# The last 64 rows of the contraction in the weight gradients gw2 and gw1 as paired 64-row matmuls

## The chip, the cores and the metric

The kernel runs on one core of one Trainium2 chip. The core has a matrix engine (PE, with weight loads shown apart as PEld), a vector engine (DVE), a scalar engine (ACT), GpSimd (POOL), a queue engine for transfers (SP), and 16 DMA engines. The metric is the device time of one execution in microseconds (us). Before the change it is 370.83 us, the median of three runs (369.65 to 373.05).

## The reference

One block of a spectral token mixer and a token MLP, forward and backward. `x` is 2048 tokens by 448 channels (d), all in bf16. Eight arrays come out: the forward result and seven gradients.

```
h  = x + irfft2(rfft2(layernorm(x)) * (w_r + i w_i))
v  = layernorm(layernorm(h))                  # the MLP norms its input again
u  = gelu(einsum("bsd,sf->bdf", v, w1) + b1)  # F = 1792
y  = einsum("bdf,fs->bds", u, w2) + b2
h2 = h + transpose(y)
outputs: h2 and the gradients of x, w_r, w_i, w1, b1, w2, b2
```

The two gradients that matter here are sums over the 448 channels:

- gw2 (`out_6`, 1792 x 2048): gelu output (f by d) times the incoming gradient (d by s).
- gw1 (`out_4`, 2048 x 1792): normed input (s by d) times the gradient ahead of the gelu (d by f).

## The kernel before

[...] 448 is three times 128 plus 64. Both gradients take the channels in four chunks of 128 rows. `ld_t4` (L187) loads a transposed operand in two DMAs: chunks 0 to 2 hold d 0 to 383, chunk 3 holds d 320 to 447, so that its first 64 rows repeat d 320 to 383. In one operand of each product those 64 rows are set to zero by a memset on POOL (`g_t` at L658, `du_t` at L712), so that they add nothing. An output tile of 128 x 512 is thus four matmuls of full height, the last of them half zeros.

The stages, with the times of the profiled execution: the forward spectral part, with the products of w2 and the incoming gradient (`dg`, L442) between its matmuls (to about 108 us); w1 with the gelu (L523, to 139); w2 (L591, to 182); the product with w1 backwards and its layernorm, sixteen blocks (L647, `norm_back`, to 228); the backward spectral part (228 to 332), in which gw2 and the first six blocks of gw1 lie between its matmuls; the rest of gw1 (332 to 364).

`gw2(j, on)` computes 128 rows of gw2: four output tiles n = 0 to 3, four matmuls each (L666). The letters of `on` say who copies each tile from PSUM to the buffer `s6`: "a" is ACT, "v" is DVE. It is "aaaa" for j = 0 and "aaav" for j = 1 to 13. Then a DMA of POOL's queue stores the rows. gw1 is sixteen blocks of the same form (L730 to L742), with three tiles of 512 columns and one of 256, all copied by ACT; the last block is stored in four pieces by SP.

The backward spectral part is a chain: `fft_rows` (L315), `fft_cols` (L333 to L347, then DVE sums L353, then L325 to L327), the complex products `cmul` on DVE (L366 to L369), `ifft_cols` (L383, L384, ACT copies L400, DVE sums L402 and L404), and `ifft_rows` with `norm_back` for sixteen rows (L413 to L422, ACT L616, DVE L619 to L622). A product of the weight gradients for w_r and w_i (`grad_w`) runs on DVE behind gw1's fourth block.

PSUM buffers come from two rings: `ps_mm` with 3 (L163: `dg`, gw2, gw1, the w1 product backwards, half of the gelu blocks) and `ps_sp` with 5 (L166: all spectral tiles, the other half). The w2 stage takes four tiles at a time from both (L588).

The order of the instructions on each engine is fixed when the program is built. A planner goes through ready instructions by priority, which is program order unless the program raises it, and gives a tile its buffer when one is free by its own estimate of the times. The backward spectral part stands ahead of gw2's blocks 1 to 13 and of gw1 in the program, so that these fill what the chain leaves. `tc.issue_after(ins)` keeps what is written under it behind `ins` on that engine's queue. On the chip each engine then runs its queue in order and waits at semaphores.

Of the kernel before, what the change touches and what calls it, by code (L numbers as in the profile page):

```python
# [17 lines left out]
P = 128  # L18
S = 2048
D = 448  # L20
# [3 lines left out]
NT = 16  # L24
# [89 lines left out]
def kernel(  # L114
# [20 lines left out]
    nc = tc.nc  # L135
    ve, ac, po, pe = nc.vector, nc.scalar, nc.gpsimd, nc.tensor
# [16 lines left out]
    def k1(shape, name, dtype=BF16):  # L153
        return ring.tile(shape, dtype, tag="k1", bufs=10, name=name)
# [5 lines left out]
        return ring.tile([P, n], dtype, tag=name, bufs=4, name=name)  # L160

    def ps_mm(shape, dtype=F32):
        return psum.tile(shape, dtype, tag="mm", bufs=3, name="ps_mm")  # L163

    def ps_sp(shape, dtype=F32):
        return psum.tile(shape, dtype, tag="sp", bufs=5, name="ps_sp")  # L166

    def ld(out, in_, eng=None):
        return (eng or nc.sync).dma_start(out=out, in_=in_)

    def st(out, in_, eng=None):
        return (eng or po).dma_start(out=out, in_=in_)  # L172

    def ld_t(out, in_):
        return nc.sync.dma_start(out=out, in_=in_, transpose=True)
# [11 lines left out]
    def ld_t4(out, in_):  # L187

        ld_t(out[:, 0:3, :], in_[:, 0:384])
        ld_t(out[:, 3, :], in_[:, 320:448])  # L190

    def ev(out, in_, on):
        if on == "a":
            return ac.copy(out=out, in_=in_)  # L194
        return ve.tensor_copy(out=out, in_=in_)
# [4 lines left out]
    def rows(ap):  # L200
        return ap.rearrange("(q h) d -> q h d", h=NT)
# [157 lines left out]
    def cmul(out, a, b, conj, done=None):  # L359
        for r0, r1 in R_GROUPS:  # L360
            n = (r1 - r0) * DF
            sl = slice(r0 * DF, r1 * DF)
            t_r = e4([P, 2, n], "t_r")
            t_i = e4([P, 2, n], "t_i")
            o_r, o_i = out(r0, r1)
            ve.tensor_tensor(out=t_r[:], in0=a[:, :, sl], in1=b[:, 0:1, sl].broadcast_to([P, 2, n]), op=ALU.mult)  # L366
            ve.tensor_tensor(out=t_i[:], in0=a[:, :, sl], in1=b[:, 1:2, sl].broadcast_to([P, 2, n]), op=ALU.mult)  # L367
            ve.tensor_tensor(out=o_r, in0=t_r[:, 0, :], in1=t_i[:, 1, :], op=ALU.add if conj else ALU.subtract)
            last = ve.tensor_tensor(out=o_i, in0=t_r[:, 1, :], in1=t_i[:, 0, :],  # L369
                                    op=ALU.subtract if conj else ALU.add)  # L370
            if done is not None:
                done(r0, r1, last)
# [201 lines left out]
    for c, sl in enumerate((0, 2, 4, 6)):  # L574
# [4 lines left out]
        t = slot(sl, [P, NFB, 512], f"w2c{c}")  # L579
# [5 lines left out]
    for t0 in range(0, NT, 4):  # L585
        hr = e4([P, 4, D], "hr")
        ld(hr[:], hn_d.rearrange("(t p) d -> p t d", p=P)[:, t0:t0 + 4, :], po)
        p2 = [ps([P, D]) for ps in ((ps_sp, ps_sp, ps_sp, ps_mm), (ps_sp, ps_sp, ps_mm, ps_mm))[t0 // 4 % 2]]  # L588
        for j in range(NFB):
            for i in range(4):  # L590
                pe.matmul(p2[i][:], lhsT=w2c[t0 // 4][:, j, i * P:(i + 1) * P], rhs=gT[:, j, :],  # L591
                          start=(j == 0), stop=(j == NFB - 1))
        for i in range(4):
            t = t0 + i
            h2 = k1([P, D], "h2")
            ve.scalar_tensor_tensor(out=h2[:], in0=p2[i][:], scalar=b2col[:, t:t + 1], in1=hr[:, i, :],  # L596
                                    op0=ALU.add, op1=ALU.add)
            h2_last = st(out_0[0][t * P:(t + 1) * P, :], h2[:])
# [31 lines left out]
    for h in range(NT):  # L630
# [3 lines left out]
        if h == 4:  # L634
            goT = slot(4, [P, 4, S], "goT")
# [7 lines left out]
        with tc.issue_after(chain[-1].ins):  # L643
            w1T_last = ld_t(w1T[:], w1Tv[h])
# [9 lines left out]

    g_t = slot(0, [P, 4, F], "g_t")
    ld_t4(g_t[:], gT_d[:])
    with tc.issue_after(h2_last.ins):
        po.memset(g_t[0:64, 3, :], 0.0)  # L658
    first = []

    def gw2(j, on):
        s6 = w4([P, S], "s6")
        for n in range(4):
            pw = ps_mm([P, 512])
            for c in range(4):
                mm = pe.matmul(pw[:], lhsT=g_t[:, c, j * P:(j + 1) * P], rhs=goT[:, c, 512 * n:512 * n + 512],  # L666
                               start=(c == 0), stop=(c == 3))
            ev(s6[:, 512 * n:512 * n + 512], pw[:], on[n])
        first.append(mm)
        return st(out_6[j * P:(j + 1) * P, :], s6[:])  # L670

    gw2(0, "aaaa")
    fft_rows(dh, zt2, 3, "aava", first[0])
    ds = slot(3, [P, 2, XW], "ds")
# [24 lines left out]
    st(out_7.rearrange("(q h) -> q h", h=NT), gb2b[:])  # L699

    for j in range(1, NFB):
        s6_st = gw2(j, "aaav")
        if j == 8:
            s6_mid = s6_st


    hlnT = slot(1, [P, 4, S], "hlnT")
    ld_t4(hlnT[:], hln_d.rearrange("h q d -> (h q) d"))
    du_t = slot(2, [P, 4, F], "du_t")
    ld_t4(du_t[:], du_d[:])  # L710
    with tc.issue_after(s6_mid.ins):
        po.memset(du_t[0:64, 3, :], 0.0)  # L712
    xs_b = slot(4, [P, 2, XW], "xs_b")


    def grad_w():
        ld(xs_b[:], xs_d[:])
        o2 = out_2.rearrange("(q r) k -> q (r k)", r=NR)
        o3 = out_3.rearrange("(q r) k -> q (r k)", r=NR)

        def out(r0, r1):
            return xs_b[:, 0, r0 * DF:r1 * DF], xs_b[:, 1, r0 * DF:r1 * DF]

        def done(r0, r1, last):
            st(o2[:, r0 * DF:r1 * DF], xs_b[:, 0, r0 * DF:r1 * DF])
            st(o3[:, r0 * DF:r1 * DF], xs_b[:, 1, r0 * DF:r1 * DF])

        cmul(out, ds, xs_b, True, done)

    for h in range(NT):  # L730
        s4 = w4([P, F], "s4")
        for n in range(4):
            wdt = 512 if n < 3 else 256
            pw = ps_mm([P, 512])
            for c in range(4):
                pe.matmul(pw[:, 0:wdt], lhsT=hlnT[:, c, h * P:(h + 1) * P],  # L736
                          rhs=du_t[:, c, 512 * n:512 * n + wdt], start=(c == 0), stop=(c == 3))
            ev(s4[:, 512 * n:512 * n + wdt], pw[:, 0:wdt], "a")
            if h == NT - 1:
                st(rows(out_4)[:, h, 512 * n:512 * n + wdt], s4[:, 512 * n:512 * n + wdt], nc.sync)  # L740
        if h < NT - 1:
            st(rows(out_4)[:, h, :], s4[:])  # L742
        if h == 3:
            grad_w()


# [28 lines left out]
```

## Time and profile before

| what | value |
|---|---|
| median of three runs | 370.83 us |
| the profiled execution | 368.86 us |
| its span on the core | 367.1 us |
| DVE busy | 236.7 us (64%) |
| ACT busy | 213.8 us (58%) |
| POOL busy | 61.3 us (17%) |
| gw2's matmuls (L666) | 224, starts 227.6 to 310.0 us |
| gw1's matmuls (L736) | 256, 192 of 512 columns and 64 of 256, starts 310.2 to 363.4 us |
| copies of 128 x 512 by ACT (L194) | mean 589 ns |
| copies of 128 x 512 of gw2 by DVE (L195) | mean 686 ns |
| memsets of `g_t` and `du_t` on POOL | 1.61 us each |

A busy time is the sum of the instructions' records. The record of a matmul is longer than the distance to the next one's start (L666: 379 ns each, but 13 of them in 2.81 us), since matmuls are pipelined; what a matmul costs a full PE is read from the distances of the starts. The granted clock is 1.00 throughout.

### The profile page before, as it was taken

How to read it: one execution, taken by the hardware profiler on the slowest of the kernel's cores; microseconds unless marked ns; L12 is line 12 of the kernel's file. 1: busy time of each engine (PE TensorE's matmuls, PEld its weight loads, DVE VectorE, ACT ScalarE, POOL GpSimd, SP SyncE). 2: the span in 40 equal slices, each digit the busy share in tenths (PEclk: the TensorE clock that was granted, in tenths of full speed). 3: DMA queues.
4: the chain of work that ended last, by engine and by line, in shares of the span. 5: the costliest groups of instructions: out<-in, count | busy, mean ns of one | idle time of the engine just before them, and what ended most of it. 6: DMA issues, size and time to landing. Idle time of an engine off the chain costs nothing.

```text
span 367.1 us, 5776 instructions
## 1 busy us (share of the span) xinstructions
PE 347.4 (95%) x2115; PEld 200.4 (55%) x2115; DVE 236.7 (64%) x562; ACT 213.8 (58%) x410; POOL 61.3 (17%) x107
## 2 busy tenths in 40 slices
PE   0898999999999999999999999999989999999996
PEld 0555666676655555555555555556655555565553
DVE  4863679887647999422267778378995666698000
ACT  3575554456649996029022245867656676787664
POOL 1000000001122112300630000101012531356211
PEclk9999999999999999999999999999999999999999
DMA  8999999996999999999989793992774444956533
GB/s 286 267 275 292 293 248 271 303 269 223 318 234 217 349 311 349 374 343 205 269 193 186 158 186 159 163 184 96 180 190 186 183 168 162 353 209 241 230 151 150
DMA packets 132524, 86.48 MB, mean 236 GB/s; under 512 B 91952, under 2 KB 123824, under 8 KB 131984
## 3 DMA queue, kind: packets, MB, share of 16 engines
q1 hardware_dynamic: 124304, 55.78, 61.5%
q0 software_dynamic: 8048, 30.31, 22.5%
q8 instruction: 16, 0.26, 0.3%
q14 instruction: 12, 0.10, 0.1%
q10 hardware_dynamic: 144, 0.03, 0.0%
HBM read 32.81 MB, written 30.76 MB: 173 GB/s over the span
## 4 chain that ended last, share of the span: by engine, by line
PE 64%; DVE 20%; ACT 9%; DMA 4%; issue 2%; ACTq 0%; DVEq 0%
PE ps_mm L736 12%; PE ps_mm L666 10%; PE ps_sp L591 7%; PE ps_mm L523 6%; PE ps_sp L523 5%; PE ps_mm L442 5%; PE ps_mm L591 4%; DMA w2T<-in_B_w_dram 3%; DVE junk L619 3%; DVE junk L621 3%; ACT v L614 3%; DVE t_r L366 2%; DVE gg L353 2%; PE ps_sp L415 2%; DVE t_i L367 2%
## 5 line engine op out<-in xcount | busy, mean ns | idle before, releaser
L194 ACT CAST s<-ps_mm 128x512 bf16<-128x512 f32 (+1 forms) x107 | 57.6, 557 | 25.6 <-PE ps_mm L666 11.1
L666 PE MATMUL ps_mm<-goT,g_t 128*128 128x512 bf16 x224 | 55.2, 379 | 1.6 <-ACT s L194 1.5
L442 PE MATMUL ps_mm<-go_nat,w2T 128*128 128x448 bf16 x224 | 50.3, 356 | 1.0 <-DMA w2T<-in_B_w_dram 1.0
L736 PE MATMUL ps_mm<-du_t,hlnT 128*128 128x512 bf16 (+1 forms) x256 | 49.6, 352 | 0.0
L647 PE MATMUL ps_mm<-du,w1T 128*128 128x449 bf16 x224 | 43.4, 353 | 0.0
L736 PEld LDWEIGHTS <-hlnT 128*128 128x128 bf16 x256 | 25.1, 98 | 22.2
L591 PE MATMUL ps_sp<-gT,w2c 128*128 128x448 bf16 x140 | 35.6, 352 | 0.0
L614 ACT ACTIVATE v<-ps_mm,nm,rstd_h 128x448 f32<-128x448 f32 x16 | 11.6, 724 | 40.2 <-DVE nm L612 40.2
L172 POOL DMA_DIRECT2D out_dram<-s x29 | 15.6, 539 | 114.0 <-ACT s L194 87.8
L591 PEld LDWEIGHTS <-w2c 128*128 128x128 bf16 x224 | 21.9, 98 | 20.5
L647 PEld LDWEIGHTS <-w1T 128*128 128x128 bf16 x224 | 21.7, 97 | 20.7
L666 PEld LDWEIGHTS <-g_t 128*128 128x128 bf16 x224 | 21.6, 97 | 20.7 <-issue 1.4
L523 PEld LDWEIGHTS <-w1c 128*128 128x128 bf16 x224 | 21.8, 98 | 20.1 <-issue 1.3
L442 PEld LDWEIGHTS <-w2T 128*128 128x128 bf16 x224 | 21.7, 98 | 16.1 <-DMA w2T<-in_B_w_dram 1.7
L353 DVE TENSOR_TENSOR gg<-ps_sp,gi 128x450 bf16<-128x450 f32 x28 | 16.2, 621 | 17.5 <-ACT gi L350 17.5
L591 PE MATMUL ps_mm<-gT,w2c 128*128 128x448 bf16 x84 | 25.0, 352 | 0.0
L523 PE MATMUL ps_mm<-hln,w1c 128*128 128x448 bf16 x112 | 23.8, 352 | 0.4 <-DVE b1col L512 0.2
L194 ACT CAST eo<-ps_sp 128x450 bf16<-128x450 f32 x32 | 17.2, 538 | 11.0 <-PE ps_sp L415 10.7
L596 DVE SCALAR_TENSOR_TENSOR h<-ps_sp,b2col,hr 128x448 bf16<-128x448 f32 x10 | 6.3, 679 | 25.7 <-PE ps_sp L591 25.7
L523 PE MATMUL ps_sp<-hln,w1c 128*128 128x448 bf16 x112 | 22.6, 352 | 0.0
L619 DVE CUSTOM_DVE_ANT_0 junk<-ps_sp,xr,rneg_x 128x448 bf16<-128x448 f32 x16 | 10.9, 682 | 16.3 <-ACT v L616 16.3
L315 PE MATMUL ps_sp<-kf,eo 128*128 128x128 bf16 x128 | 9.3, 231 | 11.9 <-DVE eo L309 11.9
(148 smaller groups left out, 622.0 us busy)
## 6 DMA issues: line engine op xcount, KB each, us to landing
w1c<-in_B_w_dram SPq DMA_DIRECT2D x7, 1024.0 KB, 8.4
w2c<-in_B_w_dram SPq DMA_DIRECT2D x8, 896.0 KB, 10.8
out_dram<-s POOLq DMA_DIRECT2D x14, 512.0 KB, 3.0
out_dram<-s POOLq DMA_DIRECT2D x15, 448.0 KB, 2.9
xs_d<-xs SPq DMA_DIRECT2D x1, 1800.0 KB, 7.7
xs_b<-xs_d SPq DMA_DIRECT2D x1, 1800.0 KB, 8.1
x<-in_A_x_dram SPq DMA_DIRECT2D x4, 448.0 KB, 4.2
go_nat<-in_grad_out_dram SPq DMA_DIRECT2D x2, 896.0 KB, 6.8
```

The source lines that it names most:

```text
L172: return (eng or po).dma_start(out=out, in_=in_)
L194: return ac.copy(out=out, in_=in_)
L353: ve.tensor_tensor(out=gg[:], in0=pr[:], in1=gi[:], op=op)
L442: pe.matmul(pg[:], lhsT=w2T[j][:, t, :], rhs=go_nat[:, t, :], start=(t == 0), stop=(t == NT - 1))
L523: pe.matmul(pu[:], lhsT=wc[:, h, o:o + P], rhs=hln[:, h, :], start=(h == 0), stop=(h == NT - 1))
L591: pe.matmul(p2[i][:], lhsT=w2c[t0 // 4][:, j, i * P:(i + 1) * P], rhs=gT[:, j, :], start=(j == 0), stop=(j == NFB - 1))
L614: ac.activation(out=v[:], in_=ps[:, 0:D], func=ACT.Identity, scale=rstd_c, bias=nm1[:])
L619: ve.tensor_tensor_reduce(out=junk[:], in0=ps[:, 0:D], in1=xhat, scale=rneg_c, scalar=0.0, op0=ALU.mult, op1=ALU.add, accum_out=nm2[:])
L621: ve.scalar_tensor_tensor(out=junk[:], in0=xhat, scalar=nm2[:], in1=v[:], op0=ALU.mult, op1=ALU.add)
L647: w1_last = pe.matmul(pd[:], lhsT=w1T[:, j, :], rhs=du[:, j, 0:D + 1], start=(j == 0), stop=(j == NFB - 1))
L666: mm = pe.matmul(pw[:], lhsT=g_t[:, c, j * P:(j + 1) * P], rhs=goT[:, c, 512 * n:512 * n + 512], start=(c == 0), stop=(c == 3))
L736: pe.matmul(pw[:, 0:wdt], lhsT=hlnT[:, c, h * P:(h + 1) * P], rhs=du_t[:, c, 512 * n:512 * n + wdt], start=(c == 0), stop=(c == 3))
```

## The change

Chunk 3 now holds the last 64 channels (d 384 to 447) twice. After the transposed load a DMA copies rows 64 to 127 of chunk 3 onto rows 0 to 63 (`ld_twice`), for all four operands, on SP's queue behind the load of w1's last block; the two memsets go. An output tile takes three matmuls of full height and one of 64 rows. Of two tiles, one uses the upper 64 rows and the other the lower 64 rows (`tails`).

`outer(first, second, ...)` fixes the order for two groups of tiles: the full matmuls of the first group, then its 64-row matmuls, then the 64-row matmuls of the second group, then the full matmuls of the second group. With `shared` the 64-row matmuls have raised priority. In gw2 and in gw1's blocks 0 to 5 the groups are tiles 0, 1 and tiles 2, 3 of one block. From block 6 on the groups are two whole blocks, the second with buffers from `ps_sp`.

The rings become 4 and 4, and the w2 stage takes two buffers from each.

```diff
     def ps_mm(shape, dtype=F32):
-        return psum.tile(shape, dtype, tag="mm", bufs=3, name="ps_mm")
+        return psum.tile(shape, dtype, tag="mm", bufs=4, name="ps_mm")
     def ps_sp(shape, dtype=F32):
-        return psum.tile(shape, dtype, tag="sp", bufs=5, name="ps_sp")
+        return psum.tile(shape, dtype, tag="sp", bufs=4, name="ps_sp")
...
+    def ld_twice(t, behind):
+        with tc.issue_after(behind.ins):
+            ld(t[0:64, 3, :], t[64:128, 3, :])
+
+    def outer(first, second, lhs, rhs, shared=True):
+        def full(outs, opens):
+            for ps, a, b in outs:
+                for c in range(3):
+                    last = pe.matmul(ps, lhsT=lhs[:, c, a], rhs=rhs[:, c, b],
+                                     start=opens and c == 0, stop=not opens and c == 2)
+            return last
+
+        def tails(outs, opens):
+            for i, (ps, a, b) in enumerate(outs):
+                k = slice(64 * (i % 2), 64 * (i % 2) + 64)
+                last = pe.matmul(ps, lhsT=lhs[k, 3, a], rhs=rhs[k, 3, b], start=opens, stop=not opens)
+            return last
+
+        last = full(first, True)
+        with tc.high_priority() if shared else nullcontext(), tc.issue_after(last.ins):
+            tails(first, False)
+            last = tails(second, True)
+        with tc.issue_after(last.ins):
+            return full(second, False)
...
-        p2 = [ps([P, D]) for ps in ((ps_sp, ps_sp, ps_sp, ps_mm), (ps_sp, ps_sp, ps_mm, ps_mm))[t0 // 4 % 2]]
+        p2 = [ps([P, D]) for ps in (ps_mm, ps_mm, ps_sp, ps_sp)]
...
-    with tc.issue_after(h2_last.ins):
-        po.memset(g_t[0:64, 3, :], 0.0)
+    ld_twice(goT, w1T_last)
+    ld_twice(g_t, w1T_last)
...
     def gw2(j, on):
         s6 = w4([P, S], "s6")
+        pws = [ps_mm([P, 512]) for n in range(4)]
+        outs = [(pws[n][:], slice(j * P, (j + 1) * P), slice(512 * n, 512 * n + 512)) for n in range(4)]
+        mm = outer(outs[:2], outs[2:], g_t, goT)
         for n in range(4):
-            pw = ps_mm([P, 512])
-            for c in range(4):
-                mm = pe.matmul(pw[:], lhsT=g_t[:, c, j * P:(j + 1) * P], rhs=goT[:, c, 512 * n:512 * n + 512],
-                               start=(c == 0), stop=(c == 3))
-            ev(s6[:, 512 * n:512 * n + 512], pw[:], on[n])
+            ev(s6[:, 512 * n:512 * n + 512], pws[n][:], on[n])
...
-    with tc.issue_after(s6_mid.ins):
-        po.memset(du_t[0:64, 3, :], 0.0)
+    ld_twice(hlnT, w1T_last)
+    ld_twice(du_t, w1T_last)
...
+    for h in range(6):
+        outs, out = gw1(h, ps_mm)
+        outer(outs[:2], outs[2:], hlnT, du_t)
+        out()
         if h == 3:
             grad_w()
+    for h in range(6, NT, 2):
+        outs, out = gw1(h, ps_mm)
+        outs_2, out_2nd = gw1(h + 1, ps_sp)
+        outer(outs, outs_2, hlnT, du_t, False)
+        out()
+        out_2nd()
```

`gw1(h, ps)` makes the four tiles of a block and the function `out`, which holds the same copies by ACT and the same stores as before.

More of the change, by code (lines that the diff above doesn't have):

```diff
@@ L701 @@
     for j in range(1, NFB):
-        s6_st = gw2(j, "aaav")
-        if j == 8:
-            s6_mid = s6_st
+        gw2(j, "aaav")
     hlnT = slot(1, [P, 4, S], "hlnT")
@@ L728, in grad_w, with gw1, out @@
         cmul(out, ds, xs_b, True, done)
-    for h in range(NT):
+    def gw1(h, ps):
         s4 = w4([P, F], "s4")
[L732 to L742, printed above, removed]
+        wdt = (512, 512, 512, 256)
+        pws = [ps([P, 512]) for n in range(4)]
+        outs = [(pws[n][:, 0:wdt[n]], slice(h * P, (h + 1) * P), slice(512 * n, 512 * n + wdt[n])) for n in range(4)]
+        def out():
+            for n in range(4):
+                cs = slice(512 * n, 512 * n + wdt[n])
+                ev(s4[:, cs], pws[n][:, 0:wdt[n]], "a")
+                if h == NT - 1:
+                    st(rows(out_4)[:, h, cs], s4[:, cs], nc.sync)
+            if h < NT - 1:
+                st(rows(out_4)[:, h, :], s4[:])
+        return outs, out
+    for h in range(6):
+        outs, out = gw1(h, ps_mm)
+        outer(outs[:2], outs[2:], hlnT, du_t)
+        out()
         if h == 3:
             grad_w()
+    for h in range(6, NT, 2):
[4 more added lines that the diff above has]
+        out_2nd()
 _INS = ['A_x', 'A_w_r', 'A_w_i', 'B_x', 'B_w1', 'B_b1', 'B_w2', 'B_b2', 'grad_out']
```

## The prediction

> **What bounds the kernel now.** I read the busy times first, then the chain of work that ended last, then the stretches of the late stages, and last single matmuls and copies in order of time.
>
> ```profile
> PE 347.4 (95%) x2115; PEld 200.4 (55%) x2115; DVE 236.7 (64%) x562; ACT 213.8 (58%) x410; POOL 61.3 (17%) x107
> ...
> PE 64%; DVE 20%; ACT 9%; DMA 4%; issue 2%; ACTq 0%; DVEq 0%
> PE ps_mm L736 12%; PE ps_mm L666 10%; PE ps_sp L591 7%; PE ps_mm L523 6%; PE ps_sp L523 5%; PE ps_mm L442 5%; PE ps_mm L591 4%; DMA w2T<-in_B_w_dram 3%; DVE junk L619 3%; DVE junk L621 3%; ACT v L614 3%; DVE t_r L366 2%; DVE gg L353 2%; PE ps_sp L415 2%; DVE t_i L367 2%
> ```
>
> PE is the bound, and gw1 and gw2 are the two largest groups of the chain. The stretches (length, then busy time of PE, PEld, DVE, ACT, POOL) show the same where the change acts:
>
> ```profile
> 276.00:310.00 34.00, 33.87 (x198) 19.17 (x197) 20.27 (x44) 22.96 (x42) 11.66 (x20) 1.00 0.47 179
> 310.00:332.00 22.00, 21.83 (x135) 13.03 (x134) 18.24 (x40) 16.60 (x34) 9.02 (x17) 1.00 0.74 268
> 332.00:363.70 31.70, 31.67 (x169) 16.30 (x167) 6.25 (x14) 21.78 (x43) 9.77 (x19) 1.00 0.50 197
> ```
>
> From 276 us to the end PE is full and nothing else is, so a matmul less is time less. One stage differs: from 254.55 to 275.8 us DVE has no gap.
>
> **What a matmul costs.** From the chain in order of time (start, length):
>
> ```profile
> 281.34 2.81 PE ps_mm L666 x13
> ```
>
> 2.81/13 = 0.216 us for 512 columns. A gw1 block takes 3.03 us (ACT copies its first tile at 340.40 and the next block's at 343.43); less 12 x 0.216 this leaves 0.109 for each of 256 columns.
>
> **What is removed.** Two 64-row matmuls beside each other take one slot instead of two. gw2: 2 x 0.216 = 0.432 a block. gw1: one pair of 512 and one of 512 with 256 save 0.216 + 0.109 = 0.325 a block. Gross: 14 x 0.432 + 16 x 0.325 = 11.2 us. No row here has two row halves at work at once, so a pair lies between one slot and two. I take one slot: the spacings above go with the columns (448 columns: 0.189, 128: 0.056), and the two halves share neither array rows nor a PSUM bank. Two slots is the slower rival.
>
> **What is added on PE.** Going to another shape of the array and back costs something, which two places show:
>
> ```profile
> 90.20 0.92 PE L442 MATMUL ps_mm<-go_nat,w2T 128*128 128x448 bf16 x4
> 91.05 0.18 PE L511 MATMUL ps_mm<-ident,b1r 14*128 14x14 bf16 x1
> 91.09 0.17 PE L511 MATMUL ps_mm<-ident,b2r 16*128 16x16 bf16 x1
> ```
> ```profile
> 231.96 1.07 PE L315 MATMUL ps_sp<-kf,eo 128*128 128x128 bf16 x16 [0.21 <-DVE eo L309]
> 232.96 0.22 PE L693 MATMUL ps_mm<-ident,sb 128*14 128x128 bf16 x1
> 233.12 0.61 PE L666 MATMUL ps_mm<-goT,g_t 128*128 128x512 bf16 x2
> ```
>
> The four L442 end their streaming at 90.20 + 4 x 0.188 = 90.95; the 14-row matmul starts at 91.05: 0.10 late. The sixteen L315 end at 232.86, L693 starts at 232.96: 0.10. L693 streams 128 columns to 233.02, L666 starts at 233.12: 0.10. Between the two small ones lie 0.04. So I price one `outer` at 0.10 in, 0.04 for the second half's start, 0.10 out: 0.24 us. Bounds: 0.04 (the loads hide as they do between full matmuls) and 0.44 (0.10 at each 64-row matmul of a gw2 block, plus the 0.04). There are 14 + 6 + 5 = 25 of them: 6.0 us of the 11.2.
>
> Net by place: gw2 0.432 - 0.24 = 0.19 a block. Block 0 does not count, for it lies in a wait for DVE (0.21 at 231.96, above, and a shorter block only lengthens it): 13 x 0.19 = 2.5. gw1 blocks 0 to 5: 6 x 0.085 = 0.5. The five double blocks: 5 x (0.65 - 0.24) = 2.05. Sum 5.05 us.
>
> **A new wait in the stage where DVE is full.** Tile 3 of every gw2 block but the first is copied by DVE, behind the spectral work. This is how those copies lie on DVE:
>
> ```profile
> 253.80 0.68 DVE L195 CAST s<-ps_mm 128x512 bf16<-128x512 f32 x1
> 254.55 0.86 DVE L366 TENSOR_TENSOR t_r<-ds,w_b 128x1350 bf16<-128x1350 bf16 x1
> ...
> 273.90 0.76 DVE L195 CAST ab<-ps_sp 128x256 bf16<-128x256 f32 x2
> 274.56 1.29 DVE L195 CAST s<-ps_mm 128x512 bf16<-128x512 f32 x2
> ```
>
> None in 20 us, then two at once. Before, the first tile stuck holds one of three buffers, and a whole further block passes through the other two: 38 matmuls of L666 run from 254.5 to 274.5. Afterwards a block needs all four buffers before its 64-row matmuls can end. With one stuck, the next block gets no further than its six first full matmuls; behind the waiting 64-row matmul on PE's queue stand its second half, and ACT waits for its first two tiles. So at most one block and six matmuls fit, 16 + 6 = 22 of the old count. The lost fill is 16 x 0.216 = 3.5 us, by the eighth that each matmul has become cheaper 3.0. The other bound is 0, if DVE's order leaves a place for one copy. I take 2.0, nearer to the upper end, since DVE's row shows no gap.
>
> **What is moved or costs nothing.** The copies: four issues on SP. SP issues `w_b` at 216.61 and 217.95 and is then free until `hlnT` at 230.22. Two issues at 1.29 us (the longer of `w_b`'s) and 6.7 us to land (as `w_b`) end at 227.7; the first 64-row matmul comes at 227.6 + 6 x 0.216 = 228.9. Cover 1.2 us; at 10.8 us (the slowest large load of the page) gw2's block 0, and behind it the last `fft_rows`, would wait 2.9 us. The copy of `hlnT` makes SP wait for the load (issued 236.5 to 243.3, 11 to 14 us to land), that of `du_t` to about 272; SP's next issues are `du_t` at 258.8, which waits for the spectral part, and `xs_b` at 310.4, which waits for gw2. The memsets lay on POOL, idle 83% of the time: nothing. PSUM rings: in `fft_cols` four tiles a step are alive and the next step's come only behind the last of them, so four are enough; `dg`, the gelu and w1's stage have a full PE, and a fourth buffer gives nothing. Bounds 0 and 1 us; I take 0. The w2 stage keeps eight buffers in two groups: 0. The end: ACT empties two blocks in a row at 0.49 us a tile (x2 in 0.86), 1.74 a block against 2.27 of PE's second half; the last tile is copied 0.2 us later than now.
>
> Sum: -5.05 + 2.0 + 0.2 = -2.85 us. The profiled execution, 368.86, would become 366.0. It lies 2.0 below the median, so I put the median at 370.83 - 2.85 = **368.0 us**.
>
> **The rivals.**
>
> *The change of shape costs next to nothing.* At 0.04 an `outer`, 25 x 0.20 = 5.0 come back; with the stuck copy too finding its place, 2.0 more: 361.0 to 363.0. For it: a 64-row load could be made ready as full ones are (PEld overlaps PE everywhere). Against: 0.10 at all three changes that the trace shows. Chance 0.21.
>
> *The stuck buffer spreads.* Every block needs both its last buffers at one instant, so PE's queue stops whenever ACT is late by more than a pair's slack, in the spectral stage above all. At 0.25 us for each of 19 shared blocks it is 4.75 us: 372.8; it begins to outweigh the gain at 0.15 a block. For it: PE already waits 0.67 us twice for ACT at 273.5 and 275.4. Against: ACT is busy 23.0 of 34 us from 276 on. Chance 0.16.
>
> *The halves don't run beside each other.* Then the change does not do what it says. The gross 11.2 is gone, switching (25 x 0.20 = 5.0), the lock (2.0) and the end (0.2) stay: 370.83 + 7.2 = 378.0. The point that decides is the distance between the starts of a pair: under 0.1 us or 0.216. Chance 0.10.
>
> *The second pair's loads wait for the first pair.* Each pair behind another in an `outer` (14 + 6 + 15 = 35) then pays a further 0.10, as at L511: 3.5 us, 371.5. Against it: sixteen L315 follow each other at 0.056 us, each with its own load. Chance 0.06. [...]
>
> [...]
>
> **How the numbers follow.** The forecast has 0.47, with its own range from 365.5 to 371 (lock 0 to 3, change of shape 0.17 to 0.31 an `outer`, copies late by 0 to 1). About 1% either way, 367.1 to 374.5, is what a measurement here can't tell from no change. Of the forecast 0.17 lies below 367.1, 0.30 within. First rival: faster, 0.21. Second: within 0.10, slower 0.06. Third: slower, 0.10. Fourth: within. Faster 0.38, same 0.46, slower 0.16. Range 361.5 to 374: it leaves out the third rival and the ends of the first and second.
>
> **What would show it.** In the changed profile: two 64-row matmuls with starts under 0.1 us apart; 0.10 us without streaming at each change of shape; L195 copies of `s` missing on DVE for some 20 us in the `ifft_cols` stage, and PE there waiting for DVE; the last full stage 5 x 0.41 = 2 us shorter; SP's copies landed before gw2 begins. It would be wrong if PE waits at the 64-row matmuls outside that stage, or if the order of the spectral part comes out otherwise, since one planner lays out both.

## The result and the profile after

| | before | after |
|---|---|---|
| median | 370.83 us (7 runs, 369.57 to 373.05) | 367.97 us (7 runs, 367.12 to 368.67) |
| ratio after to before | | 0.9926, 95% interval 0.9901 to 0.9952 |
| the profiled execution | 368.86 us | 367.25 us |
| its span | 367.1 us | 365.5 us |

The change gains 2.9 us; 368.0 was predicted. The sum came out right, but, as the experiments show, not its terms: two errors of the same size cancelled. The page of after, busy times and the chain that ended last:

```profile
PE 341.9 (94%) x2100; PEld 191.2 (52%) x2115; DVE 236.9 (65%) x562; ACT 209.1 (57%) x410; POOL 58.0 (16%) x105
...
PE 62%; DVE 20%; ACT 10%; DMA 4%; issue 3%; ACTq 0%; DVEq 0%
```

PE is still the bound, with two points less of the chain. The granted clock of the run is 0.998. In after, L202 is the full matmuls of `outer`, L209 its 64-row matmuls, L221 the copies by ACT and L222 those by DVE. The stretches, cut at the same events as before's (first `ifft_rows`, first block of gw1, end of the spectral part; length, then busy time of PE, PEld, DVE, ACT, POOL):

```profile
276.00:306.00 30.00, 29.32 (x176) 14.73 (x178) 17.22 (x38) 19.30 (x37) 9.15 (x17) 1.00 0.49 185
306.00:335.00 29.00, 28.33 (x179) 15.28 (x182) 22.09 (x48) 21.38 (x44) 10.98 (x21) 1.00 0.70 253
335.00:361.20 26.20, 24.40 (x137) 11.05 (x136) 6.45 (x15) 16.30 (x36) 8.89 (x17) 1.00 0.48 185
```

Before, PE's time in these three fell short of the stretch by 0.13, 0.17 and 0.03 us. Now it falls short by 0.68, 0.67 and 1.80, and the middle stretch has grown from 22 to 29 us. (15 of after's matmuls left no record, x2100 against 2115 weight loads, so that counts of its matmuls are a few short and a small part of the shortfall is not idle time.) The list of PE's waits of after (us in total, times, longest) names waits at a 64-row matmul and at the full ones behind it, the second and third line here, where before waited for ACT in gw2 instead (the last line, of before):

```profile
PE ps_sp L342 <- DVE eo L336: 12.3, 4, 11.0
PE ps_sp L209 <- DVE nm L646: 1.4, 1, 1.4
...
PE ps_mm L202 <- ACT s L221: 0.5, 1, 0.5
```
```profile
PE ps_mm L666 <- ACT s L194: 1.5, 3, 0.7
```

The lengths of the stages, worked out in all kernels from the starts of PE's matmuls in the order of time: from the third group of `fft_rows` (start 232) to the first `ifft_cols`, to the first `ifft_rows`, to the first block of gw1, to the last matmul of the spectral part, to PE's end, to the end of the span. The last column is PE's part, the first five together. The start itself lies between 230.73 and 233.42 us in the traces of the fourteen kernels, so spans of single traces are not compared, only PE's part and the end. "Rings" is the ring sizes and the order of the w2 stage's tiles alone; the other names are told below.

| us | to ifft_cols | to ifft_rows | to gw1 | to the last spectral | to PE's end | to the end | PE's part |
|---|---|---|---|---|---|---|---|
| before | 29.25 | 12.96 | 36.08 | 21.37 | 32.05 | 3.42 | 131.71 |
| rings alone | 29.24 | 12.75 | 34.40 | 21.79 | 31.61 | 3.41 | 129.79 |
| rings, gw2's halves | 29.49 | 13.74 | 30.95 | 28.95 | 26.64 | 3.26 | 129.77 |
| rings, gw1's halves | 29.24 | 12.75 | 34.40 | 22.68 | 29.61 | 4.36 | 128.68 |
| after | 29.48 | 13.74 | 30.95 | 28.60 | 26.11 | 4.31 | 128.88 |
| gw2 copied by ACT alone | 29.11 | 12.61 | 34.59 | 22.69 | 29.31 | 4.30 | 128.31 |
| single blocks to 8 | 29.48 | 13.74 | 30.95 | 29.08 | 23.22 | 4.33 | 126.47 |
| and the last two single | 29.49 | 13.74 | 30.95 | 29.07 | 23.43 | 3.37 | 126.68 |

From before to after: PE's part -2.83, the end +0.89, and 0.32 from a later start (232.28 against 231.96): the 1.6 us between the spans. The medians are further apart, 2.86 us, because before's profiled execution lies 2.0 below its median and after's 0.7.

### The profile page after: what moved, and what is told of

Read it like the earlier page. It is cut to its first block, busy times and chain, and to the rows that moved or that the text cites. A ratio compares the mean times of both kernels' runs of the same rounds, so it can differ in the third digit from the quotient of the medians.

```text
span 365.5 us, 5760 instructions
## 1 busy us (share of the span) xinstructions
PE 341.9 (94%) x2100; PEld 191.2 (52%) x2115; DVE 236.9 (65%) x562; ACT 209.1 (57%) x410; POOL 58.0 (16%) x105
## 4 chain that ended last, share of the span: by engine, by line
PE 62%; DVE 20%; ACT 10%; DMA 4%; issue 3%; ACTq 0%; DVEq 0%
PE ps_mm L202 11%; PE ps_mm L550 6%; PE ps_mm L618 6%; PE ps_sp L618 6%; PE ps_mm L469 6%; PE ps_sp L550 5%; DVE junk L646 4%; DVE junk L648 4%; DMA w2T<-in_B_w_dram 3%; ACT v L641 3%; PE ps_mm L209 3%; PE ps_sp L202 2%; PE ps_sp L410 2%; PE ps_sp L411 2%; PE ps_sp L352 2%
## 5 line engine op out<-in xcount | busy, mean ns | idle before, releaser
L221 ACT CAST s<-ps_mm 128x512 bf16<-128x512 f32 (+1 forms) x87 | 44.8, 569 | 22.4 <-PE ps_mm L209 14.3
L469 PE MATMUL ps_mm<-go_nat,w2T 128*128 128x448 bf16 x224 | 51.1, 361 | 1.3 <-DMA w2T<-in_B_w_dram 1.3
L202 PE MATMUL ps_mm<-goT,g_t 128*128 128x512 bf16 x159 | 40.7, 379 | 0.3
L618 PE MATMUL ps_mm<-gT,w2c 128*128 128x448 bf16 x112 | 30.4, 353 | 0.0
L618 PE MATMUL ps_sp<-gT,w2c 128*128 128x448 bf16 x112 | 30.4, 353 | 0.0
L202 PEld LDWEIGHTS <-hlnT 128*128 128x128 bf16 x192 | 18.3, 98 | 20.7 <-issue 4.8
L202 PE MATMUL ps_mm<-du_t,hlnT 128*128 128x512 bf16 (+1 forms) x127 | 26.7, 351 | 0.7 <-ACT s L221 0.5
L221 ACT CAST eo<-ps_sp 128x450 bf16<-128x450 f32 x32 | 17.3, 540 | 10.8 <-PE ps_sp L442 10.5
L202 PEld LDWEIGHTS <-g_t 128*128 128x128 bf16 x168 | 16.0, 97 | 13.9 <-issue 1.7
L646 DVE CUSTOM_DVE_ANT_0 junk<-ps_sp,xr,rneg_x 128x448 bf16<-128x448 f32 x16 | 10.9, 682 | 18.3 <-ACT v L643 18.3
L623 DVE SCALAR_TENSOR_TENSOR h<-ps_mm,b2col,hr 128x448 bf16<-128x448 f32 x8 | 5.1, 680 | 25.0 <-PE ps_mm L618 25.0
```

Of the source, the lines that this page charges most:

```text
L202: last = pe.matmul(ps, lhsT=lhs[:, c, a], rhs=rhs[:, c, b], start=opens and c == 0, stop=not opens and c == 2)
L469: pe.matmul(pg[:], lhsT=w2T[j][:, t, :], rhs=go_nat[:, t, :], start=(t == 0), stop=(t == NT - 1))
L646: ve.tensor_tensor_reduce(out=junk[:], in0=ps[:, 0:D], in1=xhat, scale=rneg_c, scalar=0.0, op0=ALU.mult, op1=ALU.add, accum_out=nm2[:])
```

## The experiments

Twelve kernels, four at a time on one chip. Each ratio is to the kernel before on the same chip (medians 369.65, 369.61 and 370.3 us); where two medians are compared, both are from the same chip or the text gives both ratios. Differences of ratios are turned into microseconds with these medians; the medians alone give up to 0.6 us less or more. After was measured apart, beside before's 370.83.

### One row half for both tiles of a pair

Both operands hold the last 64 channels in both halves, so the sums are the same; only the concurrency goes.

```
-                k = slice(64 * (i % 2), 64 * (i % 2) + 64)
+                k = slice(0, 64)
```

> Every 64-row matmul uses the upper 64 rows, so that the two of a pair share their array rows; nothing else differs from the changed kernel (both halves hold the same 64 channels, so the outputs are the same). Theory (the gain is that two halves run at once, one slot for two): the gross 11.2 us come back, of which little is hidden, 10 to 11.5 us slower than the changed kernel's 367.97, that is 378 to 379.5, ratio to before 1.02. Rival (the halves run one after the other anyway, and the gain came from the rings or the order): within 1 us of 367.97.

372.54 us, ratio 1.007 (1.0047 to 1.0093), so 5.3 us slower than after's ratio and not 10 to 11.5. The last 64-row matmuls of a double block in the order of time (start, length), first after, then this kernel:

```profile
352.14 0.60 PE L209 MATMUL ps_mm<-du_t,hlnT 64*128 64x512 bf16 x4
```
```profile
348.90 0.93 PE L209 MATMUL ps_mm<-du_t,hlnT 64*128 64x512 bf16 x4
349.66 0.92 PE L209 MATMUL ps_sp<-du_t,hlnT 64*128 64x512 bf16 x4
```

Four of them, one with 256 columns, take 0.76 us from start to start here, which is 3 x 0.216 + 0.109, and 0.34 in after, where the next one starts on the half that had the 256 columns. The single starts are 0.216 us apart here; in after the two of a pair start 0.002 to 0.004 us apart. So the pairs run at the same time and the rival "the halves don't run beside each other" is out. But about half of what the pairs save is not seen in the time. By the profiles PE's part is 5.88 us longer than after's (134.76 against 128.88), the end 0.72 shorter (3.59 against 4.31), and no wait of `ps_sp` for L646 is left in the list of PE's waits. After pays for its speed with a wait and a longer end which this slower kernel doesn't have; they are 1.4 and 0.7 us, and the rest of the difference is not placed.

### The second group's halves after its full matmuls

Two changes of shape each way in an `outer` where after has one.

```
-            tails(first, False)
-            last = tails(second, True)
+            last = tails(first, False)
...
-            return full(second, False)
+            last = full(second, True)
+        with tc.high_priority() if shared else nullcontext(), tc.issue_after(last.ins):
+            return tails(second, False)
```

> The 64-row matmuls of the second group stand behind its full matmuls instead of ahead of them, so that each group makes its own change of shape: 25 more trips into the 64-row shape and back. Theory (a trip costs the 0.09 in and 0.10 out that the trace after the change shows between full and 64-row matmuls): 25 x 0.19 = 4.8 us slower, 372.8. By the prediction's 0.24 a trip it would be 6.0 us, 374. Rival (a change of shape costs next to nothing, 0.04): 1 us, 369.

369.33 us, ratio 0.9986 (0.996 to 1.0012): 2.2 us slower than after by the two ratios, not 4.8. The price of a change was as expected. In the order of time of this kernel two blocks of gw1:

```profile
346.43 2.44 PE L202 MATMUL ps_mm<-du_t,hlnT 128*128 128x512 bf16 x11
348.81 0.60 PE L209 MATMUL ps_mm<-du_t,hlnT 64*128 64x512 bf16 x4
349.34 2.44 PE L202 MATMUL ps_sp<-du_t,hlnT 128*128 128x512 bf16 x12
351.72 0.60 PE L209 MATMUL ps_sp<-du_t,hlnT 64*128 64x512 bf16 x4
```

One block takes 348.81 to 351.72 = 2.91 us: nine full matmuls of 512 and three of 256 are 2.275, two slots of pairs 0.432, which leaves 0.20 for going there and back. Part of what went better than expected is a wait: PE's wait for `nm` at `ps_sp` is 0.4 us here, 1.4 in after. And the stage from `ifft_cols` to `ifft_rows` is 12.72 us long, 13.74 in after. Again a slower order paid less elsewhere.

### gw2's fourth tile copied by ACT

The theory of the stuck DVE tile by itself: the wait is taken away by giving all of gw2's copies to ACT.

```
-        gw2(j, "aaav")
+        gw2(j, "aaaa")
```

> In gw2's blocks 1 to 13 ACT copies the fourth tile too, instead of DVE. Theory of the prediction (a copy stuck on DVE locks the next block out of PE for 2.0 us): 2 us faster, 366.0. Rival A (no lock, since tiles 0 and 1 free two buffers through ACT before tile 3 needs one, as the trace shows; only its 64-row matmuls get scattered, three of them alone, two groups of three and one of two, some five further trips of 0.19 and two slots of 0.216): 1.0 to 1.5 us faster, 366.5 to 367. Rival B (ACT, with 13 copies of 0.49 us more, makes the chain late): slower by up to 2 us.

366.83 us, ratio 0.9908 (0.9878 to 0.9939). After has 0.9926 (0.9901 to 0.9952): this is 0.7 us less, which the intervals can't tell from nothing, and not 2.0. The profile of after says why. DVE's copies in the order of time:

```profile
254.35 0.68 DVE L222 CAST s<-ps_mm 128x512 bf16<-128x512 f32 x1
275.80 1.88 DVE L222 CAST s<-ps_mm 128x512 bf16<-128x512 f32 x3
```

DVE is shut for 20 us, as predicted, and three tiles come out at once. So three of four buffers were stuck in the end, and PE did not stop: from 254.5 to 274.5 it ran 26 matmuls of L202 and 12 of L209, 38 on record, where before ran 38 of gw2 and the kernel with the rings alone 42 in the same stretch of its stage. That is four fewer at most, not the 16 of the prediction. What it pays shows in the same stage's 64-row matmuls, first of after, then of this kernel:

```profile
265.35 0.60 PE L209 MATMUL ps_mm<-goT,g_t 64*128 64x512 bf16 x3
...
266.41 0.37 PE L209 MATMUL ps_mm<-goT,g_t 64*128 64x512 bf16 x1
...
272.72 0.39 PE L209 MATMUL ps_mm<-goT,g_t 64*128 64x512 bf16 x2
...
273.78 0.37 PE L209 MATMUL ps_mm<-goT,g_t 64*128 64x512 bf16 x1
...
274.41 0.39 PE L209 MATMUL ps_mm<-goT,g_t 64*128 64x512 bf16 x1
```
```profile
265.26 0.60 PE L209 MATMUL ps_mm<-goT,g_t 64*128 64x512 bf16 x4
...
273.31 0.60 PE L209 MATMUL ps_mm<-goT,g_t 64*128 64x512 bf16 x4
```

Where a buffer is missing, a block's four 64-row matmuls come in two or three goes with `ifft_cols` between them: each go pays its own change of shape (in after 0.096 us going in and 0.093 coming out, by the medians), and a lone one is not paired. With ACT's copies they come four together, and the stage is 12.61 us long instead of 13.74. But PE's part is only 0.57 shorter in all, since the stages behind it got longer.

### Single blocks of gw1 up to block 8

In after, blocks 6 and 7 of gw1 are the first double block, which takes eight buffers while the last rows of the spectral part still use `ps_sp`. Here blocks 6 and 7 are single.

```
-    for h in range(6):
+    for h in range(8):
...
-    for h in range(6, NT, 2):
+    for h in range(8, NT, 2):
```

> gw1's blocks 6 and 7 are single blocks too, and the double blocks begin at 8. Theory (block 7's buffers from ps_sp are still held by the last spectral row; PE waits 1.44 us for DVE and 0.46 for ACT, and 0.5 more when block 9 meets ACT): these 2.4 us go, less 0.2 for one more trip, 365.8. Rival (the end of the spectral part makes PE wait wherever the double blocks begin): within 0.5 us of 367.97.

364.87 us, ratio 0.9855 (0.9823 to 0.9887): 2.6 us below what after's ratio gives. The wait is gone from the list, and PE's part is 2.4 us shorter: 2.9 less behind the last spectral matmul, for 0.5 more ahead of it. In after that place looks like this (PE in the order of time):

```profile
332.82 2.10 PE L202 MATMUL ps_mm<-du_t,hlnT 128*128 128x512 bf16 x8 [0.46 <-ACT s L221]
...
335.24 0.60 PE L209 MATMUL ps_sp<-du_t,hlnT 64*128 64x512 bf16 x3
...
338.25 0.27 PE L209 MATMUL ps_sp<-du_t,hlnT 64*128 64x256 bf16 x1 [1.44 <-DVE nm L646]
338.45 2.44 PE L202 MATMUL ps_sp<-du_t,hlnT 128*128 128x512 bf16 x12
```

Block 7's last tile waits for the `ps_sp` buffer of the last spectral row, until `norm_back` on DVE (L646) has read it; the wait for it and the one at 332.82, 1.44 + 0.46, make 1.9 of the 2.4 us; the rest is not placed. That the 64-row matmuls of a double block all stand ahead of the second block's full ones is what makes PE wait: there is other work, but it is queued behind them. In after's chain of waits, followed back from the end, the pieces ahead of that place are DVE's, and not `norm_back`'s alone: `xs_b` (L396) is one of the products of `grad_w`, which stand between the last rows:

```profile
333.44 0.60 DVE junk L646
...
337.20 0.39 DVE xs_b L396
337.59 0.59 DVE junk L646
338.25 0.27 PE ps_sp L209
```

Of the chain from 325 to 340 us these products (L393 to L396) hold some 45%, `norm_back` on DVE a third. Giving `grad_w` a later place might shorten the wait too; that was not run.

### The rings alone

Before, with the rings of 4 and 4 and the new order of the w2 stage's tiles, and no 64-row matmul. The prediction has 0 for this.

```
-        return psum.tile(shape, dtype, tag="mm", bufs=3, name="ps_mm")
+        return psum.tile(shape, dtype, tag="mm", bufs=4, name="ps_mm")
...
-        return psum.tile(shape, dtype, tag="sp", bufs=5, name="ps_sp")
+        return psum.tile(shape, dtype, tag="sp", bufs=4, name="ps_sp")
...
-        p2 = [ps([P, D]) for ps in ((ps_sp, ps_sp, ps_sp, ps_mm), (ps_sp, ps_sp, ps_mm, ps_mm))[t0 // 4 % 2]]
+        p2 = [ps([P, D]) for ps in (ps_mm, ps_mm, ps_sp, ps_sp)]
```

> The kernel before with nothing changed but the PSUM rings (4 and 4) and the w2 stage's two buffers from each; no 64-row matmuls. Theory (the prediction's zero for the rings): within 0.5 us of the kernel before. Rival (the spectral part needs its fifth buffer, and the rings ate part of the gain): 1 to 2 us slower than before.

Not as expected: 367.3 us, ratio 0.9924 (0.99 to 0.9949). The rings alone gain 2.8 us (1.9 to 3.7; 2.3 by the two medians), which can't be told from the whole change; PE's part in the trace is 1.92 us shorter. The stretch in which DVE is full looks different, first before, then the rings alone, whose stage starts 0.78 us later:

```profile
255.00:275.00 20.00, 18.93 (x128) 12.15 (x126) 20.00 (x37) 12.13 (x24) 2.15 (x4) 1.00 0.74 187
```
```profile
255.78:275.78 20.00, 19.86 (x134) 12.72 (x132) 20.00 (x37) 12.69 (x25) 2.15 (x4) 1.00 0.71 188
```

DVE is just as full, but PE gets six matmuls more in. The two waits of 0.67 us for ACT's copy `s` that before has at 273.5 and 275.4 are not in this kernel's list; they make 1.35 of the 1.92 us. Whether their going is the cause is tested below.

### gw2's halves alone

The rings and the new gw2; gw1 and its operands as before. Against the kernel before, beside the lines above:

```
-        po.memset(g_t[0:64, 3, :], 0.0)
+    ld_twice(goT, w1T_last)
+    ld_twice(g_t, w1T_last)
...
+        mm = outer(outs[:2], outs[2:], g_t, goT)
```

> The rings and gw2 as changed, gw1 as before (four full matmuls a tile, the memset of du_t back). Theory after the first runs (gw2's saving is lost in the stages up to ifft_rows, where the trace after the change is 0.23 + 0.78 us longer than before, and only the seven or so blocks behind it pay, 0.23 each): 0.5 to 1 us faster than before. By the prediction's terms 2.5 - 2.0 = 0.5 us faster. Rival (gw2 carries the gain, the scattered 64-row matmuls cost little): 2 us or more faster.

367.39 us, ratio 0.9938 (0.9913 to 0.9963), against 367.3 with the rings alone on the same chip: gw2's halves alone add nothing that can be measured. The table of stages says how: 1.24 us longer up to `ifft_rows` and 1.26 shorter behind it. Up to `ifft_rows` cheaper matmuls save nothing. The spectral chain with DVE full in it seems to set the pace there, and the scattered 64-row matmuls come between the matmuls of the chain; this is a reading of the traces, not tested by itself.

### gw1's halves alone

The rings and the new gw1; gw2 as before. Against the kernel before, beside the rings:

```
-        po.memset(du_t[0:64, 3, :], 0.0)
+    ld_twice(hlnT, w1T_last)
+    ld_twice(du_t, w1T_last)
...
+    for h in range(6):
...
+    for h in range(6, NT, 2):
```

> The rings and gw1 as changed, gw2 as before (the memset of g_t back). Theory: gw1's six single blocks pay 0.13 each and the double blocks 0.45 each, 3.0 in all; the wait for ps_sp's buffers is there only if the spectral part ends behind block 6 again. With that wait (2.4) and the later end (0.9) the sum is 0.3 us slower than before, without the wait 2.1 us faster. By the prediction's terms 2.05 + 0.5 - 0.2 = 2.35 us faster.

366.94 us, ratio 0.9913 (0.9884 to 0.9941). Against the rings alone 0.4 us, within the intervals; PE's part is 1.11 us shorter, and the end, 4.36 against 3.41, takes 0.95 of it back. The wait for the last row is there without gw2's halves:

```profile
334.77 0.27 PE L209 MATMUL ps_sp<-du_t,hlnT 64*128 64x256 bf16 x1 [1.23 <-DVE nm L646]
```

### The last block's stores over two queues

The version with single blocks to 8, where ACT empties the last two blocks one after the other and SP issues the four last stores behind them. Here the even ones go by POOL.

```
-                    st(rows(out_4)[:, h, cs], s4[:, cs], nc.sync)
+                    st(rows(out_4)[:, h, cs], s4[:, cs], nc.sync if n % 2 else po)
```

> As the run with single blocks up to 8, and the last block's four stores go to POOL's queue (tiles 0 and 2) and SP's (tiles 1 and 3) in turn. Theory (the end is 0.9 us longer than before because ACT now copies the last four tiles 0.49 us apart and SP issues a store every 0.58 us, so that the last store is issued 0.5 us after its copy): 0.4 us faster than the run with single blocks up to 8. Rival (the end is the landing of the last store, whatever queue): the same, or slower by 0.5 to 1 us if a store of POOL's queue lands last.

Slower, where 0.4 us faster was expected: 366.23 us, ratio 0.9895 (0.9867 to 0.9923). By the ratios that is 1.5 us above single blocks to 8, which ran on another chip. PE's part is as long as there (126.48 us against 126.47), but the span ends 5.68 us behind it, not 4.33. The last stores in the order of time (start, length of issue), first with SP alone, then with two queues:

```profile
357.59 0.54 POOL L172 DMA_DIRECT2D out_dram<-s  x1 [3.32 <-ACT s L221]
357.82 2.31 SPq L172 DMA_DIRECT2D out_dram<-s  x4
```
```profile
357.35 1.07 POOL L172 DMA_DIRECT2D out_dram<-s  x2 [3.33 <-ACT s L221]
358.06 1.10 SPq L172 DMA_DIRECT2D out_dram<-s  x2
358.82 0.54 POOL L172 DMA_DIRECT2D out_dram<-s  x1 [0.40 <-ACT s L221]
```

The last issue does start earlier, at 358.82 and 358.83 instead of 359.55, and the last store lands at 361.61 instead of 361.74, so neither is what makes the end later. It is a DRAIN instruction on POOL that begins with POOL's last store (length least, median and longest in ns; first and last start in us), again with SP alone first:

```profile
L809 POOLq DRAIN  x3: 46/103/4374, 357.6 to 362.5; - x3
```
```profile
L809 POOLq DRAIN  x3: 51/103/4254, 358.8 to 363.6; - x3
```

The long one is the first. With SP alone it runs from 357.57 to 361.95, with two queues from 358.80 to 363.05, though the store behind which it began had landed 1.44 us earlier; in both kernels the span ends 0.78 to 0.79 us behind it. POOL's last store starts 0.81 us ahead of PE's end in the one and 0.66 behind it in the other, and the end moves by about as much.

### Before, with gw2 copied by ACT alone

If the rings gain by the DVE tile that holds one of three buffers, then taking that tile away from DVE should gain without them. The stage starts 1.31 us later than in the kernel before.

```
-        s6_st = gw2(j, "aaav")
+        s6_st = gw2(j, "aaaa")
```

> The kernel before, rings 3 and 5, with one thing changed: in gw2's blocks 1 to 13 ACT copies the fourth tile instead of DVE. Theory (the rings' gain comes from the stage where DVE is full: two tiles wait there for DVE's copy, which leaves gw2 one of three buffers, and PE waits 1.5 us for ACT; a fourth buffer leaves two): the same gain without a fourth buffer, 1.5 to 2 us faster than before, ratio 0.995. Rival (the rings gain elsewhere, in the forward part or by the planner's order): within 0.5 us of before.

370.31 us, ratio 1.0004 (0.9982 to 1.0027): nothing. PE waits for ACT's `s` 0.2 us here instead of 1.5 and is busier in the DVE-full stretch,

```profile
256.31:276.31 20.00, 19.45 (x129) 12.42 (x130) 19.19 (x35) 13.19 (x25) 3.06 (x6) 1.00 0.95 202
```

but PE's part is 131.70 us, as before's 131.71. Up to gw1 the stages are 0.68 us shorter, and the last is 0.64 longer: less of gw1 was done ahead of it. ACT, which in the next stretch, 275 to 311, now works 27.4 of 36 us (before 23.3 of 35, from 275 to 310), may be what takes the gain, but no wait of that size is named. So the theory is not confirmed: with three buffers, a tile that doesn't get stuck is worth nothing here, though most of the waiting for ACT is gone, and what a fourth buffer does beyond it stays open.

### gw1's halves with single blocks to 8

Does gw2's part pay once the wait at the first double block is gone? gw1's halves alone, as above, with

```
-    for h in range(6):
+    for h in range(8):
...
-    for h in range(6, NT, 2):
+    for h in range(8, NT, 2):
```

> The rings and gw1's 64-row matmuls with single blocks up to 8; gw2 as before (its memset back). Theory (rings 2.8, eight single blocks 0.13 each, four double blocks 0.45 each, less 0.9 at the end: 4.7 us; gw2's 64-row matmuls gain nothing net): 4.7 us faster than before, ratio 0.987, as near as can be told to the 5.3 of the run with both. Rival (gw2's 64-row matmuls pay some 2 us once PE no longer waits for ps_sp): 3.3 us faster, 0.991.

366.57 us, ratio 0.9903 (0.987 to 0.9936). With gw2's halves as well, it was 0.9855 (0.9823 to 0.9887). The intervals just overlap; the middle lies 1.8 us apart by the ratios, 1.05 by each median's distance from before on its chip, and PE's part 0.93 (127.40 against 126.47). So gw2's halves probably do pay here, while with the double blocks from 6 they did not: what they free behind `ifft_rows` is then no longer lost to the wait (an inference; the runs show the sums only).

### The last two blocks single

As single blocks to 8, and blocks 14 and 15 by themselves, one from each ring, so that ACT does not have two blocks to empty at the end.

```
-    for h in range(8, NT, 2):
+    for h in range(8, NT - 2, 2):
...
+    for h in (NT - 2, NT - 1):
+        outs, out = gw1(h, (ps_mm, ps_sp)[h % 2])
+        outer(outs[:2], outs[2:], hlnT, du_t, False)
+        out()
```

> All changed, single blocks up to 8, and blocks 14 and 15 single again with buffers from ps_mm and ps_sp, without raised priority. Theory (the later end comes from ACT emptying two blocks at a stretch and SP's stores then queueing): the end from PE's last matmul shrinks from 4.3 to about 3.5 us at the price of one trip more, 0.20: 0.6 us faster than the run with single blocks up to 8, ratio 0.984. Rival (the landing of the last store sets it): 0.2 us slower.

363.91 us, ratio 0.9831 (0.9803 to 0.9859), the fastest of all: 6.3 us below before, and 3.5 below after by the two ratios. The end is 3.37 us instead of 4.33, for 0.21 more on PE. The last rows of ACT, POOL and SP in the order of time, first after, then this kernel:

```profile
359.92 1.89 ACT L221 CAST s<-ps_sp 128x512 bf16<-128x512 f32 x4
360.36 0.54 POOL L172 DMA_DIRECT2D out_dram<-s  x1 [3.33 <-ACT s L221]
360.58 2.31 SPq L172 DMA_DIRECT2D out_dram<-s  x4
```
```profile
356.81 0.54 POOL L172 DMA_DIRECT2D out_dram<-s  x1 [2.35 <-ACT s L221]
357.58 1.84 ACT L221 CAST s<-ps_sp 128x512 bf16<-128x512 f32 x4 [1.07 <-issue]
...
358.20 1.84 SPq L172 DMA_DIRECT2D out_dram<-s  x4
```

In after, ACT comes to the last block straight from the one before it; here it stands idle for 1.07 us between them. Two things follow. SP issues its fourth store 0.50 us behind ACT's copy in after, 0.20 here. And POOL's store of block 14, with the DRAIN of 4.2 to 4.4 us behind it, starts 0.81 us ahead of PE's end in after, 1.99 here. In after both paths are through at the same time (POOL's DRAIN at 364.69, SP's at 364.64), so both had to become shorter. The intervals of this kernel and the one with singles to 8 overlap (0.9831 and 0.9855); the end in the two traces does tell them apart.

### The last two single, gw2 copied by ACT

```
-        gw2(j, "aaav")
+        gw2(j, "aaaa")
```

> As the run with the last two blocks single, and ACT copies all of gw2's tiles. Theory (no 64-row matmul is scattered any more in the stage where DVE is full; it gave 0.7 us when done alone): 0.5 to 1 us faster than that run, ratio 0.982. Rival (13 more copies make ACT late for the spectral chain): the same or slower.

365.27 us, ratio 0.9857 (0.9834 to 0.988), 1.4 us above the kernel without it on the same chip. The 1.5 us that ACT's copies save up to `ifft_rows` (41.72 against 43.23) come back with more behind it: PE's part is 127.54 us against 126.68, and its waits for ACT's `eo` are 1.4 us here against 0.7. What gained little in after costs here.

## Why the prediction was right, and where it was not

The time was right by luck: the rings, put at 0, gained about what all the other terms together, put at -2.85, did not. By the prediction's own steps:

**The pairs and the price of a change of shape: right.** The two of a pair start 0.002 to 0.004 us apart ("under 0.1" was asked for). The median of the 60 changes in after, worked out from the starts, is 0.096 us going in and 0.093 coming out; going there and back is 0.20 us by the two-trips kernel and by the double blocks, where 0.24 was taken. A double block takes 349.78 to 355.39 = 5.61 us, 5.65 predicted. The next pair starts 0.226 us behind the one ahead of it, a slot being 0.216, so the fourth rival is out too. Behind a tile of 256 columns the halves get out of step: the second block's four start at 352.48, 352.59, 352.70 and 352.80, the first of them 0.109 us, the time of 256 columns, behind that tile and while the other half still streams 512. The second pair uses the same two row halves as the first, and of the 0.096 us of a change of shape only 0.010 lies between the pairs. For one slot the prediction names halves that share neither array rows nor a PSUM bank; no run shows the banks, and before the change none showed a pair. What the runs show is the starts: 0.002 to 0.004 us apart in after, 0.216 apart where both tiles of a pair use the same rows.

**"PSUM rings: 0": the term that was most mis-sized.** It measured -2.8 us (1.9 to 3.7; 2.3 by the medians). The prediction looked at `fft_cols`, `dg`, the gelu and the w2 stage, and not at gw2, although it names, for the rival of the stuck buffer, the very wait that is gone with the fourth buffer (0.67 us twice, at 273.5 and 275.4), and counts one of three buffers as stuck. Only a part of the 2.8 is placed: 1.68 us in the stage from `ifft_rows` to gw1, 0.2 ahead of it and nothing net behind; PE's part is 1.9 shorter in the trace. The cause is not shown: with ACT's copies and three buffers those waits shrink from 1.5 to 0.2 us as well, and nothing is gained.

**"Net by place, -5.05", with the lock and the end -2.85: about nothing in the time.** From the rings alone to after PE's part falls by 0.91 us and the end rises by 0.90. Three steps failed:

- The first double block's wait for the last spectral row was not in the sum at all. PE stands for 1.9 us there, and 2.4 to 2.6 are gained where the double blocks begin at 8. The prediction had taken gw1's part by the count of matmuls, five double blocks in a full PE; but the first of them takes its `ps_sp` buffers while the last spectral row still holds one: the chain there runs through DVE, `norm_back` and `grad_w`, not through PE. The wait is there with gw2 as before too (1.23 us). The prediction's own sign of being wrong, PE waiting at 64-row matmuls outside the DVE-full stage, is this one.
- "gw2: 13 x 0.19 = 2.5" is 0 in after. Up to `ifft_rows`, where these blocks fill what the chain leaves, the path became 1.24 us longer, and 1.26 shorter behind it.
- "The last tile is copied 0.2 us later": the end is 0.89 longer. The step was right as far as it went: the last copy ends 0.64 us behind PE's end instead of 0.46. It left out what follows. SP issues the last store 0.50 us behind its copy instead of 0.18, and the store lands 2.18 us later instead of 1.62. Just as late is POOL's DRAIN behind block 14's store, which starts 0.81 us ahead of PE's end instead of 2.27.

**"The lock, +2.0": the wrong mechanism.** With up to three tiles stuck PE still ran 38 matmuls of gw2 on record, as before, against 42 with the rings alone. The step assumed that a block holds four buffers from start to end; its first two tiles end and are emptied by ACT while the other two wait. The cost is in the scattered 64-row matmuls instead, 1.13 us in `ifft_cols`, most of which is hidden later: 0.7 us are gained by the ratios when it is removed, which can't be told from nothing.

**The copies: right in time, wrong in the landing.** SP issued the two sooner than was taken (0.54 and 0.59 us, not 1.29) and they took longer to land. From the list of DMA issues of after (KB each, us from issue to landing):

```profile
goT<-goT SPq DMA_DIRECT2D x1, 256.0 KB, 9.6
hlnT<-hlnT SPq DMA_DIRECT2D x1, 256.0 KB, 2.8
...
g_t<-g_t SPq DMA_DIRECT2D x1, 224.0 KB, 9.9
du_t<-du_t SPq DMA_DIRECT2D x1, 224.0 KB, 3.4
```

6.7 was taken. The copy of `g_t` lands at 228.83, behind the start of gw2 and not ahead of it; the first 64-row matmul, at 229.30, follows the last full one at the usual 0.096 us and does not wait. 0.47 of the cover of 1.2 us was left; with gw2's halves alone the copy did come late, and PE waited 0.2 us. The distance between the second and third group of `fft_rows` is 5.26 us, 5.27 before, so it costs nothing there.

**The rivals.** "The change of shape costs next to nothing" is out by the 0.20 us. "The stuck buffer spreads" came true in one point only: PE does wait at a 64-row matmul outside the DVE-full stage, at one place and not at nineteen, and for a `ps_sp` buffer.

**What stays open.** Why the rings gain: the trace places 1.9 of the 2.8 us, and the edit meant to gain the same without them gained nothing. Why POOL's DRAIN goes on for more than a microsecond behind the landing of the store. And how much of the wait at the first double block is due to `grad_w`'s products on DVE.

## What to carry to other kernels

Price a change of ring sizes by itself, at every stage that uses the ring; here the rings alone gained as much, within the intervals, as the whole change. Work that fills the gaps of a chain may save nothing by becoming shorter, as gw2's halves alone did here: look at what lies at the end of the chain, and give the first step that needs all buffers to a place where the chain has ended. Measure a composite change in its parts: two reorderings of this one (single blocks to 8, the last two single) are worth 3.5 us, more than the 2.9 of the change itself.

## What was not expected of the hardware

- Two copies of 256 and 224 KB from one half of a chunk to the other took 9.6 and 9.9 us to land beside w1's and `w_b`'s loads, and 2.8 and 3.4 us for the same sizes later.
- A change between 128-row and 64-row matmuls costs 0.09 to 0.10 us each way in after with one, four or eight 64-row matmuls between, so a lone pair (one slot of 0.216 saved, 0.19 paid) is worth almost nothing, and four 64-row matmuls in one go about 0.23 (both worked out from these figures).
- Behind its last store POOL has a DRAIN of 4.14 to 4.37 us in all fourteen traces, longer than the store takes to land (by 1.44 us with two queues). With two of the last block's four stores by POOL instead of SP it began later, and the span ended 1.35 us later behind PE's end.
- In after the two row halves went on each by itself: behind a tile of 256 columns one half began its next 64-row matmul 0.10 us ahead of the other (352.48 and 352.59).
